# Scores and AV of two head pairs at a time in a sparse-attention and gated-MLP kernel

## The chip, the cores and the metric

The kernel runs on one core of a Trainium2 chip. A core has a matrix engine (TensorE; PE in the profile, with its weight loads as PEld), a vector engine (DVE), a scalar engine for activations (ACT), GpSimd (POOL) and SyncE (SP). Each takes its instructions in its own order and waits for others by semaphores. DMA transfers are issued by SP, ACT and POOL and carried by 16 DMA engines. The metric is the time of one execution in microseconds (us).

## The reference, cut to what matters

For 4 batches, 8 heads, 768 rows and 64 columns: each row attends to the rows less than 16 away and to 24 block summaries (the maximum of the keys and the mean of the values of 32 rows, each with the weight of a whole block). The result goes through a two-layer MLP.

```python
k_sum = k.reshape(B, H, nb, block, D).max(axis=3)          # block 32, nb 24
v_sum = v.reshape(B, H, nb, block, D).mean(axis=3)
scores_l = scale * (q @ k.T)                               # kept where |i - j| < 16
scores_s = scale * einsum('bhsd,bhnd->bhsn', q, k_sum) + log(block)
a = softmax(concat([where(mask_l, scores_l, -1e9), scores_s], -1))
out = a @ concat([v, v_sum], axis=2)
x = out.transpose(0, 2, 1, 3).reshape(B * S, H * D)        # 3072 x 512
h = x @ w_in                                               # 512 -> 2048
y = (h * sigmoid(beta * h)) @ w_out                        # 2048 -> 512
```

## The kernel before, in words

**Attention.** Heads are worked in four pairs (g = 0 to 3), two heads side by side on the partitions. The 768 queries of a head are cut into 12 chunks of 64: six positions m by two parities. A chunk needs only a window of 96 keys, and the 24 summaries stand behind them, so one weight tile `kw[:, par, m]` of 128 columns holds both. The scores of a chunk are one matmul of 128 x 64 per head. An exponential on ACT takes the scores from PSUM to `attn`, a multiplication on DVE with `band` sets what lies outside the window to zero (`mask`), and AV multiplies by `ve` or `vo`: rows of V laid out at an offset for the two parities, a column of ones for the softmax's sum, and the block means in the partitions from 96 on (`mean_v` makes them, `rows_v` copies them in for a pair). `norm` on DVE divides by the sum and writes `x_nat`, and `x_transpose` brings `x_nat` into `xT`, the MLP's input. It does so by PE transposes in batch 0 and for pairs 2 and 3 of batch 1, by a DMA transpose on SP's queue elsewhere.

**MLP.** `h_group` multiplies `w_in` by `xT` (h_ps, then a Silu on ACT), `o_part` multiplies by `w_out` (o_ps, a quarter of a row of 128 tokens at a time, then a copy and a store). Batch 0 is done in two halves (units 0 and 1, 8 h groups each), the others whole (units 2, 3 and 4, 16 groups each).

**PSUM.** Its eight banks are three double banks (tag `big`: scores, AV, h groups) and two single ones (tag `t`: o_ps, some transposes). A buffer is used again when its last reader is done.

**What sets the order.** The program is written out by hand for each engine. Within a batch b the h groups (one each 1.3 of schedule time) and then the o parts (0.865 each) form the main list; `up` is the time at which the o parts begin. Everything else, above all the attention of batch b+1, is put between them with `at_time(t, f, ...)`: a function is written out in front of the first main item whose time is not below t; those with equal t keep the order in which they were named. These are places in the program, not times on the chip. At a batch's end the first two h groups of the next batch begin with three of their four parts (contraction over pairs 0 to 2), and the fourth follows.

**Loads.** Queries, keys and values come by POOL's queue, and after batch 0 also `cross`, which brings keys and queries into place by DMA transposes on SP's queue (`kw`, `qt`); `copy_v` makes `vo` from `ve`. For batches 2 and 3, `load_next` loads a pair's values, keys and queries a whole batch ahead. Its first call also sets a column of `ve` with a memset on DVE, and the large load of values behind it waits for that memset.

Of the kernel before, what the change touches and what calls it, by code (L numbers as in the profile page):

```python
# [12 lines left out]
def kernel(  # L13
# [243 lines left out]
    def kw_of(b, g):  # L257
        return kw_bufs[(b * npair + g) % NKW]
# [109 lines left out]
    def scores_half(g, hf, late=False):  # L368
# [16 lines left out]

        if hf == 0:
            if g % 2 == 0:
                at[(0, g)] = at_pool.tile([P, 2, HM, 2, 2, QT], bf16, name="attn", tag="attn", bufs=3)
            at[(0, g, 0)] = a = at[(0, g - g % 2)][:, g % 2]
            out = a.rearrange("p m h r f -> p h m (r f)")  # L390
            src = big[:, :, 0:2 * HM * QT].rearrange("p h (m f) -> p h m f", f=2 * QT)
        else:
            a = at_pool.tile([P, HM, 2, 2, QT], bf16, name="attn01", tag="attn01", bufs=4)
# [33 lines left out]
    def scores(b, g, par):  # L427
        kw, q = kw_of(b, g), qt_bufs[g]
        if par == 0:
            at[(b, g)] = at_pool.tile([P, 2, nch, 2, QT], bf16, name="attn", tag="attn", bufs=3)  # L430
        a = at[(b, g)][:, par]
        big = ps.tile([P, 2, 512], f32, name="s_ps", tag="big", bufs=3)
        sv = big[:, :, 0:nch * QT].rearrange("p h (m f) -> p h m f", f=QT)
        for m in range(nch):
            for h in range(2):
                lo = h * D
                nc.tensor.matmul(sv[:, h, m], kw[lo:lo + D, par, m, :], q[lo:lo + D, m, par], start=True, stop=True)  # L437
        nc.scalar.activation(out=a.rearrange("p m h f -> p h m f"), in_=sv, func=ACTF.Exp, scale=scale)  # L438

    def mask(b, g, par):  # L440
        a = at[(b, g)][:, par]
        nc.vector.tensor_mul(out=a, in0=a, in1=band[:, par])  # L442

    def av(key, m0, n, tag="big"):
        b, g = key[:2]
        a = at.pop(key)
        if tag == "t":
            o = psum([P, 2, n * VW], f32, "av_ps", "t")
        else:
            o = ps.tile([P, 2, 512], f32, name="av_ps", tag="big", bufs=3)[:, :, 0:n * VW]  # L450
# [177 lines left out]
    for b in range(B):  # L628
# [22 lines left out]
        if nxt == 1:  # L651
            first, step = up + 0.3, 4.4
            for g in pairs:
                t = first + step * g
                p = (up - 9.0, up - 4.5, up + 7.5, up + 8.6)[g]
                if g < 2:
                    at_time(p, prep_k, 1, g, "t")
                    at_time(p + 0.8, prep_q, 1, g, "t", dve)
                    at_time(p + 0.8, copy_v, 1, g)
                else:  # L660
                    at_time(up + 0.5, cross, 1, g)
                    at_time((up + 4.0, up + 6.1)[g - 2], copy_v, 1, g, 0, nch, act)
                at_time(p, top_k, 1, g)
                at_time(p if g < 3 else first + step * 2 + 0.7, rows_k, 1, g)
                for par in range(2):
                    at_time(t, scores, 1, g, par)
                    at_time(t, mask, 1, g, par)
                at_time((up + 2.7, up + 2.7, up + 8.55, first + step * 2 + 0.8)[g], rows_v, 1, g)
                a = t + (4.3 if g == 0 else 3.5)
                at_time(a, av, (1, g), 0, nch)  # L670
                at_time(a, norm, (1, g), nch)
                at_time(a + (0.1 if g < 2 else 2.9), x_transpose, (1, g), 0, nch, "big", dve)
            at_time(up + 2.6, mean_v, 1, pairs, "big")
        elif nxt is not None:
# [10 lines left out]
            for g in range(npair + 1):  # L685
                t = up + 4.0 * g
# [76 lines left out]
```

## Time and profile before

| | us |
|---|---|
| runs of the kernel | 216.63, 216.89, 214.6 (median 216.63) |
| the profiled execution | 214.79, with a span of 213.1 |
| TensorE busy | 206.5 (97%) |
| ACT, DVE, POOL busy | 118.2, 89.4, 66.1 |
| o_ps matmuls (400) | 86.5 busy |
| h_ps matmuls (512) | 86.3 busy |
| scores L437 (288) and AV L455 (336) | 6.3 and 16.8 busy |
| masks L442 (24) | 13.1, 0.556 each |
| exponentials L438 (24) | 18.1, 0.808 each |

Busy times of matmuls overlap, since each is counted from its start to its end and the next begins before that; the chain of work that ended last shows what each adds. In the chain a row gives the start, the length, the engine, the tile and line, and the number of instructions that stand behind each other. In a row of the timeline the brackets at the end give how long the engine was idle before it and who ended that. The landing time of a DMA runs from its issue to its last byte.

By the span's start: batch 0's h groups run to 48.0, its o parts to 74.3; batch 1's h groups from 74.63, batch 2's from 121.13, batch 3's from 167.64.

### The profile page before, as it was taken

The page shows a single profiled execution, that of the slowest core. Times are in us where ns is not written, and L with a number is a line of the kernel's source. Part 1 is how long each engine was busy: PE and PEld are TensorE (multiplying, and loading weights), DVE is VectorE, ACT ScalarE, POOL GpSimd, SP SyncE. Part 2 cuts the span into 40 slices and gives each one's busy share as a digit, 9 for nine tenths or more (in the row PEclk, how much of TensorE's full clock was granted, in tenths as well). Part 3 has the DMA queues.
Part 4 walks back from the last instruction along what each step waited for, and adds up shares of the span by engine and source line. Part 5 has one row for each costly group of instructions (what it writes and reads, how often), then busy time and mean ns, then how long its engine had stood idle before and what let it go on. Part 6 is the DMA issues. An engine that isn't in the chain of part 4 may idle for free.

```text
span 213.1 us, 4886 instructions
## 1 busy us (share of the span) xinstructions
PE 206.5 (97%) x2024; PEld 113.7 (53%) x2024; DVE 89.4 (42%) x233; ACT 118.2 (55%) x165; POOL 66.1 (31%) x88
## 2 busy tenths in 40 slices
PE   7799999999999999999999999999999999999992
PEld 2466666654445565554554455555554556654452
DVE  4487773495798211249644123605454000002121
ACT  3699767879753177668352377678342477740000
POOL 7985345343198483069890000000000000000000
PEclk9999999999999999999999999999999999999999
DMA  6999999999999999999999976721333400001222
GB/s 173 181 154 191 205 204 206 184 178 164 160 133 196 198 221 157 170 150 150 181 150 176 221 156 129 139 40 49 89 86 89 137 0 3 0 0 57 91 86 65
DMA packets 93622, 28.34 MB, mean 133 GB/s; under 512 B 82256, under 2 KB 90656, under 8 KB 93600
## 3 DMA queue, kind: packets, MB, share of 16 engines
q0 software_dynamic: 63184, 13.24, 76.8%
q1 hardware_dynamic: 29968, 14.26, 33.0%
q10 hardware_dynamic: 448, 0.52, 0.7%
q8 instruction: 16, 0.26, 0.5%
q14 instruction: 6, 0.05, 0.1%
HBM read 27.27 MB, written 6.29 MB: 158 GB/s over the span
## 4 chain that ended last, share of the span: by engine, by line
PE 91%; DMA 3%; DVE 2%; issue 1%; POOL 0%; POOLq 0%
PE o_ps L521 40%; PE h_ps L500 39%; PE av_ps L455 4%; DMA q_run<-in_q_dram 3%; PE s_ps L437 3%; PE vm_ps L340 1%; PE px L479 1%; DVE km L293 1%; PE pq L279 1%; PE pk L279 1%; PE av_ps L411 1%; PE av_ps L418 1%; PE s_ps L383 1%; PE beta_ps L332 1%; PE s_ps L378 0%
## 5 line engine op out<-in xcount | busy, mean ns | idle before, releaser
L521 PE MATMUL o_ps<-w_out_sb,h_sb 128*128 128x512 bf16 (+2 forms) x400 | 86.5, 371 | 0.0
L500 PE MATMUL h_ps<-xT,w_in_sb 128*128 128x384 bf16 x512 | 86.3, 326 | 0.0
L507 ACT ACTIVATE h_sb<-h_ps,beta_sb 128x768 bf16<-128x768 f32 (+1 forms) x80 | 59.4, 772 | 24.3 <-PE h_ps L500 24.2
L500 PEld LDWEIGHTS <-w_in_sb 128*128 128x128 bf16 x512 | 49.1, 98 | 32.3 <-issue 0.2
L521 PEld LDWEIGHTS <-h_sb 128*128 128x128 bf16 x400 | 37.0, 98 | 40.9
L541 ACT COPY o_sb<-o_ps 128x512 f32<-128x512 f32 x18 | 10.6, 587 | 31.0 <-PE o_ps L521 19.9
L438 ACT ACTIVATE attn<-s_ps 128x768 bf16<-128x768 f32 x24 | 18.1, 808 | 8.6 <-PE s_ps L437 8.6
L442 DVE TENSOR_TENSOR attn<-attn,band 128x768 bf16<-128x768 bf16 x24 | 13.1, 556 | 20.6 <-ACT attn L438 19.3
L541 DVE COPY o_sb<-o_ps 128x512 f32<-128x512 f32 x5 | 3.5, 692 | 38.5 <-PE o_ps L521 38.5
L118 POOL DMA_DIRECT2D ve<-in_v_dram x12 | 14.4, 1196 | 16.3 <-PE h_ps L500 10.9
L111 POOL DMA_DIRECT2D k_nat<-in_k_dram x20 | 16.8, 843 | 7.5 <-DMA w_out_sb<-in_moe_w_out_dram 4.7
L111 POOL DMA_DIRECT2D q_nat<-in_q_dram x20 | 16.6, 836 | 7.9 <-DMA ve<-in_v_dram 3.8
L465 DVE TENSOR_TENSOR x_nat<-av_ps,r 128x768 bf16<-128x768 f32 (+1 forms) x20 | 15.9, 797 | 0.7
L311 DVE TENSOR_TENSOR half<-kw 128x384 bf16<-128x384 bf16 x8 | 2.9, 358 | 29.8 <-DMA kw<-k_nat 29.8
L293 DVE TENSOR_REDUCE km<-kw 128x24 bf16<-128x768 bf16 x8 | 7.6, 948 | 5.4 <-ACT kw L289 5.3
L464 DVE RECIPROCAL r<-av_ps 128x12 f32<-128x12 f32 (+1 forms) x20 | 4.3, 215 | 10.9 <-PE av_ps L455 9.5
L455 PEld LDWEIGHTS <-attn 128*64 128x64 bf16 x336 | 6.7, 111 | 3.9 <-issue 2.8
L455 PE MATMUL av_ps<-ve,attn 128*64 128x65 bf16 x168 | 8.5, 197 | 0.1
L455 PE MATMUL av_ps<-vo,attn 128*64 128x65 bf16 x168 | 8.3, 197 | 0.0
L437 PEld LDWEIGHTS <-kw 64*128 64x128 bf16 x288 | 4.9, 95 | 4.5 <-issue 4.0
L399 ACT ACTIVATE attn<-s_ps 128x768 bf16<-128x768 f32 x8 | 6.0, 808 | 1.1 <-PE s_ps L383 0.9
L437 PE MATMUL s_ps<-qt,kw 64*128 64x64 bf16 x288 | 6.3, 191 | 0.0
(92 smaller groups left out, 140.1 us busy)
## 6 DMA issues: line engine op xcount, KB each, us to landing
out_dram<-o_sb SPq DMA_DIRECT2D x23, 256.0 KB, 3.0
w_out_sb<-in_moe_w_out_dram POOLq DMA_DIRECT2D x4, 512.0 KB, 17.2
k_nat<-in_k_dram POOLq DMA_DIRECT2D x20, 96.0 KB, 8.2
q_nat<-in_q_dram POOLq DMA_DIRECT2D x20, 96.0 KB, 7.8
w_in_sb<-in_moe_w_in_dram POOLq DMA_DIRECT2D x3, 512.0 KB, 13.4
ve<-in_v_dram POOLq DMA_DIRECT2D x6, 192.0 KB, 7.3
vo<-ve SPq DMA_DIRECT2D x10, 97.5 KB, 5.5
ve<-in_v_dram POOLq DMA_DIRECT2D x2, 384.0 KB, 12.8
```

The costliest lines, as they stand in the source:

```text
L111: nc.gpsimd.dma_start(out=t[:, :, h], in_=(k_row if nm == "k" else q_row)[b, g, :, h])
L118: nc.gpsimd.dma_start(out=ve_bufs[b % 2][:, lo:hi, 0:D], in_=src)
L293: nc.vector.tensor_reduce(out=km_of[g], in_=keys_of(b, g).rearrange("p (n f) -> p n f", f=block), op=ALU.max, axis=mybir.AxisListType.X)
L437: nc.tensor.matmul(sv[:, h, m], kw[lo:lo + D, par, m, :], q[lo:lo + D, m, par], start=True, stop=True)
L438: nc.scalar.activation(out=a.rearrange("p m h f -> p h m f"), in_=sv, func=ACTF.Exp, scale=scale)
L442: nc.vector.tensor_mul(out=a, in0=a, in1=band[:, par])
L455: nc.tensor.matmul(ov[par * QT:(par + 1) * QT, h, m], a[:, par, m, h], t[:, PC * g + nch * h + m0 + m], start=True, stop=True)
L465: nc.vector.tensor_mul(out=x.rearrange("p m h d -> p h m d"), in0=ov[:, :, :, 0:D], in1=r[:, :, :, None].to_broadcast([P, 2, n, D]))
L500: nc.tensor.matmul(big[:, j, 0:MG], w_in_sb[:, ki, ni * P:(ni + 1) * P], xT[b][:, ki, tok:tok + MG], start=(ki == 0), stop=(ki == k1 - 1))
L507: nc.scalar.activation(out=hb.rearrange("p (k m) -> p k m", m=MG), in_=big[:, j:j + w, 0:MG], func=ACTF.Silu, scale=beta_sb[:, ni:ni + 1])
L521: nc.tensor.matmul(o_ps[:, c0:c1], h_bufs[(u, ni * w // k2)][:, ni % (k2 // w), ms * P:(ms + 1) * P], w_out_sb[:, ni, c0:c1], start=(ni == ...
L541: (nc.scalar.copy if u + 1 < len(units) else nc.vector.tensor_copy)(out=o_sb[:], in_=o_ps[:])
```

## The change

Scores of batches 1 to 3 are written for two pairs at once (`scores(b, g0)`): 24 chunks of two heads in three PSUM tiles that fill both banks, and three exponentials of 128 x 1024 in place of four of 128 x 768. `mask` takes a whole pair, 1536 columns, in place of a half. AV of the two pairs of a call follows one on the other, then their two norms. In batch 0 `av_pair` puts AV of two pairs into the two halves of one double bank, where each pair had a single bank. The tiles of `attn` are laid out anew for this (two of four pairs or of two pairs, in place of three and four smaller ones). The times in the schedule change with it, and so do two others: `prep_q` of batch 1 stands next to `prep_k`, and the loads of batch 3 go from 8.0 + 3.5 g to 16.0 + 3.0 g.

```diff
+        if g == 0:
+            at[hf] = at_pool.tile([P, npair, HM, 2, 2, QT], bf16, name="attn", tag="attn", bufs=2)
+        a = at[hf][:, g]
...
-    def scores(b, g, par):
-        kw, q = kw_of(b, g), qt_bufs[g]
-        if par == 0:
-            at[(b, g)] = at_pool.tile([P, 2, nch, 2, QT], bf16, name="attn", tag="attn", bufs=3)
-        a = at[(b, g)][:, par]
-        big = ps.tile([P, 2, 512], f32, name="s_ps", tag="big", bufs=3)
-        sv = big[:, :, 0:nch * QT].rearrange("p h (m f) -> p h m f", f=QT)
-        for m in range(nch):
-            for h in range(2):
-                lo = h * D
-                nc.tensor.matmul(sv[:, h, m], kw[lo:lo + D, par, m, :], q[lo:lo + D, m, par], start=True, stop=True)
-        nc.scalar.activation(out=a.rearrange("p m h f -> p h m f"), in_=sv, func=ACTF.Exp, scale=scale)
+    def scores(b, g0):
+        a = at_pool.tile([P, 2, 2, nch, 2, QT], bf16, name="attn", tag="attn", bufs=2)
+        tiles = [(g, par, m) for g in (g0, g0 + 1) for par in range(2) for m in range(nch)]
+        flat = a.rearrange("p g r m h f -> p (g r m) h f")
+        n = len(tiles) // 3
+        for j in range(3):
+            sv = ps.tile([P, 2, n * QT], f32, name="s_ps", tag="big", bufs=3).rearrange("p h (c f) -> p h c f", f=QT)
+            for c, (g, par, m) in enumerate(tiles[j * n:(j + 1) * n]):
+                for h in range(2):
+                    lo = h * D
+                    nc.tensor.matmul(sv[:, h, c], kw_of(b, g)[lo:lo + D, par, m, :], qt_bufs[g][lo:lo + D, m, par],
+                                     start=True, stop=True)
+            nc.scalar.activation(out=flat[:, j * n:(j + 1) * n].rearrange("p c h f -> p h c f"), in_=sv, func=ACTF.Exp,
+                                 scale=scale)
+        for i in range(2):
+            at[(b, g0 + i)] = a[:, i]
...
+    def av_pair(g0):
+        big = ps.tile([P, 2, 512], f32, name="av_ps", tag="big", bufs=3)
+        for i in range(2):
+            av((0, g0 + i, 1), HM, HM, big[:, i, 0:2 * HM * VW].rearrange("p (h x) -> p h x", h=2))
...
-                t = 2.0 + 2.0 * g
-                at_time(t - 1.4, mask_half, g)
-                at_time(t - 1.4, rows_v, 0, g, HM, nch)
-                at_time(t, av, (0, g, 1), HM, HM, "t")
+                t = 3.9 if g < 2 else 6.5
+                at_time(0.6 + 1.3 * g, mask_half, g)
+                at_time(0.6 + 1.3 * g, rows_v, 0, g, HM, nch)
+                if g % 2 == 0:
+                    at_time(t, av_pair, g)
                 at_time(t, norm, (0, g, 1), HM)
-                at_time(t + 1.9, x_transpose, (0, g, 1), HM, HM, "t", dve)
+                at_time(t + 2.6, x_transpose, (0, g, 1), HM, HM, "t", dve)
...
+            for g0, t, r, a, xt in ((0, up + 0.3, up + 3.4, up + 7.7, 0.1), (2, up + 12.9, up + 12.9, up + 17.2, 2.6)):
+                at_time(t, scores, 1, g0)
+                for f in (rows_v, mask):
+                    for g in (g0, g0 + 1):
+                        at_time(r, f, 1, g)
+                for g in (g0, g0 + 1):
+                    at_time(a, av, (1, g), 0, nch)
+                for g in (g0, g0 + 1):
+                    at_time(a, norm, (1, g), nch)
+                    at_time(a + xt, x_transpose, (1, g), 0, nch, "big", dve)
...
-            for g in range(npair + 1):
-                t = up + 4.0 * g
-                if g < npair:
-                    for par in range(2):
-                        at_time(t, scores, nxt, g, par)
-                        at_time(t, mask, nxt, g, par)
-                if g:
-                    at_time(t, av, (nxt, g - 1), 0, nch)
-                    at_time(t, norm, (nxt, g - 1), nch)
-                    at_time(t, x_transpose, (nxt, g - 1), 0, nch, "big", dve)
+            for g0, t, a in ((0, up + 0.8, up + 5.9), (2, up + 9.0, up + 14.5)):
+                at_time(t, scores, nxt, g0)
+                for g in (g0, g0 + 1):
+                    at_time(t, mask, nxt, g)
+                    at_time(a, av, (nxt, g), 0, nch)
+                for g in (g0, g0 + 1):
+                    at_time(a, norm, (nxt, g), nch)
+                    at_time(a, x_transpose, (nxt, g), 0, nch, "big", dve)
...
-                    at_time(up + 6.0 + 0.01 * (g + 1) if b == 0 else 8.0 + 3.5 * g, load_next, nxt + 1, g)
+                    at_time(up + 6.0 + 0.01 * (g + 1) if b == 0 else 16.0 + 3.0 * g, load_next, nxt + 1, g)
```

Two places in the written order. The first is on DVE, beside batch 1's h groups, in front of the first masks of batch 2. Before, the memset of batch 3's loads (`ve_82`; `ve_81` and `vo_83` belong to batch 2) stood ahead of pair 2's keys (`kw_87`):

```order
L699 MEMSET ve_82 32x48
L311 TENSOR_TENSOR half<-kw_87 128x384
L313 TENSOR_REDUCE km_114<-half 128x24
L319 COPY kw_87<-kw_87 128x6x96
L320 COPY kw_87<-km_114 128x2x6x24
L347 COPY vm_116<-vm_ps 128x130
L353 COPY ve_81<-vm_116 32x780
L353 COPY vo_83<-vm_116 32x780
```

In the change, at the same place of the program:

```order
L320 COPY kw_87<-km_114 128x2x6x24
L347 COPY vm_116<-vm_ps 128x130
L353 COPY ve_81<-vm_116 32x780
L353 COPY vo_83<-vm_116 32x780
L353 COPY ve_81<-vm_116 32x780
L353 COPY vo_83<-vm_116 32x780
L708 MEMSET ve_82 32x48
L353 COPY ve_81<-vm_116 32x780
```

The memset has moved behind pair 2's keys, the mean of the values (`vm_116`) and the copies of two pairs.

The second is SP's queue beside batch 1's o parts, from the second half of batch 2's attention to the first copies for batch 3. Before, a store of an o row stood between two transposes into `xT`:

```order
L474 DMA_TRANSPOSE xT<-x_nat_1936 128x6x128
L542 DMA out_dram<-o_sb 128x512
L474 DMA_TRANSPOSE xT<-x_nat_2017 128x6x128
L542 DMA out_dram<-o_sb 128x512
L474 DMA_TRANSPOSE xT<-x_nat_2071 128x6x128
L542 DMA out_dram<-o_sb 128x512 x2
L328 DMA vo_84<-ve_82 64x780
```

In the change:

```order
L483 DMA_TRANSPOSE xT<-x_nat_1868 128x6x128
L551 DMA out_dram<-o_sb 128x512 x3
L483 DMA_TRANSPOSE xT<-x_nat_2032 128x6x128
L483 DMA_TRANSPOSE xT<-x_nat_2037 128x6x128
L551 DMA out_dram<-o_sb 128x512 x2
L328 DMA vo_84<-ve_82 64x780
```

The transposes of pairs 2 and 3 (the last two into `xT` in each) stand one behind the other, with two stores behind them as the last one had before.

More of the change, by code (lines that the diff above doesn't have):

```diff
@@ L384, in scores_half @@
                              start=True, stop=True, tile_position=(lo, SUM))
+        if g == 0:
+            at[hf] = at_pool.tile([P, npair, HM, 2, 2, QT], bf16, name="attn", tag="attn", bufs=2)
+        a = at[hf][:, g]
         if hf == 0:
[L387 to L389 removed]
+            at[(0, g, 0)] = a
             out = a.rearrange("p m h r f -> p h m (r f)")
@@ L663 @@
                 at_time(p, top_k, 1, g)
-                at_time(p if g < 3 else first + step * 2 + 0.7, rows_k, 1, g)
-                for par in range(2):
[L666 to L673, printed above, removed]
+                at_time(p, rows_k, 1, g)
+            at_time(up + 3.4, mean_v, 1, pairs, "big")
+            for g0, t, r, a, xt in ((0, up + 0.3, up + 3.4, up + 7.7, 0.1), (2, up + 12.9, up + 12.9, up + 17.2, 2.6)):
[8 more added lines that the diff above has]
+                    at_time(a + xt, x_transpose, (1, g), 0, nch, "big", dve)
         elif nxt is not None:
```

21 lines of the change are left out of this document (8 added, 13 removed).

## The prediction

> **What bounds the kernel now.** I read the table of busy times first, then the chain that ended last, in order of time, and then how long single DMAs took to land.
>
> ```profile
> PE 206.5 (97%) x2024; PEld 113.7 (53%) x2024; DVE 89.4 (42%) x233; ACT 118.2 (55%) x165; POOL 66.1 (31%) x88
> ...
> PEclk9999999999999999999999999999999999999999
> ```
>
> TensorE is busy for 97% of the span, its clock granted in full; no other engine passes 55%. Whether it streams or waits, the chain tells (start, length, what, how many matmuls).
>
> ```profile
> 9.10 0.28 PE s_ps L378 x12
> ...
> 25.05 0.31 PE av_ps L455 x12
> 25.36 1.41 PE h_ps L500 x8
> 26.76 0.17 PE px L479 x3
> 26.93 1.30 PE h_ps L500 x8
> 28.23 0.36 PE av_ps L455 x12
> ...
> 30.21 0.52 PE av_ps L455 x12
> ...
> 74.63 14.30 PE h_ps L500 x88
> ...
> 100.93 0.46 PE s_ps L437 x24
> 101.39 0.50 PE av_ps L455 x24
> 101.89 4.42 PE o_ps L521 x20
> ...
> 107.27 3.56 PE o_ps L521 x16
> ...
> 121.13 14.30 PE h_ps L500 x88
> ```
>
> (L378 is scores of batch 0, L437 those of the other batches, L455 AV, L500 the first product h, L521 the second, o; px are transposes.) Two things are to be seen. From 30 us to the end the pieces join without a gap: 88 h matmuls in 14.30 are 0.1625 each at both batches, so there is no wait on that path for the change to remove; only the matmuls themselves and the cost of changing from one kind to another are left. And that cost can be read. For o_ps, 20 matmuls took 4.42 and 16 took 3.56: 0.215 each, and 0.12 more whenever o_ps follows scores or AV. For h_ps, 8 matmuls took 1.41 after AV and 1.30 after px: 0.11. For AV, 24 matmuls took 0.50 and 12 took 0.31: 0.19 for each further dozen, 0.12 for beginning. For scores, 0.46 and 0.28: 0.18 a dozen, 0.10 for beginning. So TensorE gains only by beginning less often, and loses whatever new wait is put into its stream.
>
> **The change part by part.** By these prices 48 AV matmuls in a row cost 0.50 + 2 x 0.19 = 0.88 in place of 2 x 0.50, and 48 scores 0.46 + 2 x 0.18 = 0.82 in place of 2 x 0.46.
>
> *Batch 0.* Four AV pieces (0.31, 0.36, 0.52 and the last like the first, 1.50 in all) become two of 0.50: 0.5 saved. Two returns to h_ps at 0.11 go too, and so does one more with prep_q of pair 1, now next to its prep_k, with its beginning: about 0.4 together. The 0.52 holds a short wait for DVE's rows at 29.9 to 30.2, which goes. I take 1.0. What could be late next: the first av_pair comes at about 25.05 + 1.30 = 26.35 and wants the masks and rows_v of two pairs.
>
> ```profile
> 23.39 0.49 DVE L425 TENSOR_TENSOR attn<-attn,band 128x768 bf16<-128x768 bf16 x1
> 24.82 3.03 ACT L507 ACTIVATE h_sb<-h_ps,beta_sb 128x384 bf16<-128x384 f32 x6 [0.63 <-PE h_ps L500]
> ```
>
> DVE begins them at 23.39; a mask takes about half a microsecond, and the rows_v of half the chunks take at most the 0.65 that a whole pair takes below, so it is through by 23.39 + 2 x 1.15 = 25.7. AV now takes one of the three double banks of the h groups, the one that two Silus of half a microsecond leave at 25.8. Nothing waits for more than 0.1.
>
> *Attention of batch 1* (beside batch 0's o rows). Four scores pieces become two (0.20 saved), four AV become two (0.24), and returns to o_ps, counted along the schedule, fall from eight to five (0.36); 0.8, of which I take 0.7, as one return after px costs nothing before either.
>
> *Attention of batches 2 and 3* (beside the products of batches 1 and 2). Each saves 0.20 and 0.24 as above and one return of five: 0.56.
>
> The sum without any new wait is 1.0 + 0.7 + 2 x 0.56 = 2.8 us.
>
> *ACT and DVE of two pairs.* Two exponentials of 768 took 1.51, 0.76 each; one of 1024 lies between 0.76 and 0.76 x 4/3 = 1.01, and I take 0.90. A mask of 1536 I price as two of 768, which took 1.02.
>
> ```profile
> 97.01 1.28 ACT L438 ACT_TABLE_LOAD   x1
> 98.31 1.51 ACT L438 ACTIVATE attn<-s_ps 128x768 bf16<-128x768 f32 x2
> 102.65 1.02 DVE L442 TENSOR_TENSOR attn<-attn,band 128x768 bf16<-128x768 bf16 x2
> ```
>
> Let X be the start of batch 1's h groups, 74.63 in the trace of before. Batch 2's first scores, now one o piece into the o rows, end at X+23.1, the three exponentials at X+26.4 (the table load ends at X+23.7 as before), and the masks, two of 1.0, the first from the second exponential on, at X+27.6. AV comes six o pieces after scores, at X+23.1+5.28 = X+28.4: 0.8 us of cover. Behind the masks on DVE stand max_k and rows_k of pair 3 (1.5) and then the norms; the norms end at X+31.6, and the next scores want their banks at X+32.9. The o_ps copy of the first row waits behind the exponentials until X+27.0, and its bank is wanted only after X+31. All of that I cost at nothing; if DVE came a microsecond late, AV would wait 0.2 of it, and a second microsecond in full.
>
> *The loads of batch 3.* Here is the part that I do not cost at nothing. The loads are moved from 8.0 to 16.0 of the schedule, and DVE's memset, which frees the tile for the first large load, moves past max_k and rows_k of pair 2, the mean of V and two rows_v.
>
> ```profile
> 91.46 0.10 DVE L699 MEMSET ve<- 32x48 bf16 x1 [0.22 <-issue]
> 92.45 1.05 POOL L118 DMA_DIRECT2D ve<-in_v_dram  x1 [10.94 <-PE h_ps L500]
> 95.95 0.23 DVE L347 CAST vm<-vm_ps 128x130 bf16<-128x130 f32 x1
> ...
> 136.43 0.37 DVE L353 COPY ve<-vm 32x780 bf16<-32x780 bf16 x1
> ...
> 137.08 0.37 DVE L353 COPY ve<-vm 32x780 bf16<-32x780 bf16 x1
> ...
> L111 POOL DMA_DIRECT2D q_nat<-in_q_dram x2: 838/843/848, 110.1 to 110.9; - x2
> DMA to landing us min/median/max: 8.7/8.7/8.8
> ```
>
> Before, the memset at 91.46 let the loads start at 92.45, X+17.8; the last issue, at 110.9, landed 8.8 later, at X+45.1. In the changed order the memset follows the cast (95.95 to 96.18) and the rows_v of two pairs, 0.65 each without POOL beside them (136.43 to 137.08): X+22.9. SP's work for the batch starts 0.3 later against X, as px now stands ahead of the last o part, and a load begins about 1 after its memset: loads from about X+24.2. With the 18.5 us of before from the first issue to the last they are issued until X+42.7 and land until X+51. In that time SP must bring batch 2's x of pairs 2 and 3 into xT by DMA transpose, and batch 2's first h group needs it. How long such a transpose takes to land, beside loads and alone:
>
> ```profile
> L474 SPq DMA_TRANSPOSE xT<-x_nat x1: 1215/1215/1215, 109.9 to 109.9; - x1
> DMA to landing us min/median/max: 7.7/7.7/7.7
> ...
> L474 SPq DMA_TRANSPOSE xT<-x_nat x1: 1212/1212/1212, 118.0 to 118.0; - x1
> DMA to landing us min/median/max: 3.7/3.7/3.7
> ...
> L474 SPq DMA_TRANSPOSE xT<-x_nat x1: 1237/1237/1237, 151.0 to 151.0; - x1
> DMA to landing us min/median/max: 2.7/2.7/2.7
> ...
> L474 SPq DMA_TRANSPOSE xT<-x_nat x1: 2333/2333/2333, 61.0 to 61.0; - x1
> DMA to landing us min/median/max: 8.8/8.8/8.8
> ...
> 116.75 0.23 DVE L464 RECIPROCAL r<-av_ps 128x12 f32<-128x12 f32 x1 [2.36 <-PE av_ps L455]
> 117.02 0.96 DVE L465 TENSOR_TENSOR x_nat<-av_ps,r 128x768 bf16<-128x768 f32 x1
> ```
>
> The last transpose before was issued at 118.01 for a batch that starts at 121.13; it landed in 3.7, as the loads were nearly through, and TensorE never saw it. After the change AV of pairs 2 and 3 starts at X+39.0 (scores at X+32.9, six o pieces on), pair 2's norm takes 0.23 and 0.96 and SP issues its transpose at X+40.8, pair 3's at X+42.1 behind it. That is 16.6 us after the loads began; the row of 109.9 stood 17.5 after them and took 7.7. Seven o pieces after AV batch 2's h groups begin, at X+46.0, and its third matmul, at X+46.3, needs pair 2: 5.5 after the issue. With 7.6 it lands at X+48.4, a **wait of 2.1**; pair 3's, at X+49.7, is then wanted at 48.4 + 10 x 0.1625 = X+50.0 and adds nothing. The ends of this unknown are 2.7 and 3.7 (no wait) and 8.8, the slowest transpose into xT of the trace (3.3 of wait); I take 7.6, from the row nearest in place.
>
> The Trainium skill, "DMA: Bandwidth & Descriptors", section "Queues, rings and completion order", says that a DMA engine serves its queues in turn, a packet from each. By that, beside one other queue a transpose would need about 2 x 2.7 = 5.4, an estimate from the alone row, and the wait would be nil; the row at 109.9 says 7.7, and I go by the row.
>
> At the start of batch 3's h groups no loads run; the 2.7 holds there, and nothing waits.
>
> **Sum.** The profiled execution took 214.79 (span 213.1 and 1.7 around it): 214.79 - 2.8 + 2.1 = 214.1. Two of the three runs shown (216.63 and 216.89) lie about 1.9 above it and one (214.6) beside it, and no view tells what the other kind does. The change has no part in that; I put the forecast halfway, at 214.1 + 0.9 = **215.0**.
>
> **The rivals.**
>
> 1. *The transposes land in time.* Speaks for it: the 3.7 at 118.0, when the last loads were still landing, and that the loads may be through sooner, with batch 2's transposes of keys no longer beside their first ones. Against: the rows of 7.7 and 8.8. It decides at 5.5 us. Time: 214.79 - 2.8 = 212.0, 1.3% faster.
>
> 2. *The transposes land much later, and the change is slower.* Two stand one behind the other in SP's queue, where before an o row lay between. The place is the third matmul of batch 2's h groups; from 8.3 us to landing the wait eats the whole 2.8. With the 12.9 of the slowest load of batch 2 beside its transposes (issued at 80.1), the wait is 40.8 + 12.9 - 46.3 = 7.4 and the time 214.79 - 2.8 + 7.4 = 219.4.
>
> ```profile
> L111 POOL DMA_DIRECT2D q_nat<-in_q_dram x2: 826/832/838, 79.3 to 80.1; - x2
> DMA to landing us min/median/max: 10.3/11.6/12.9
> ```
>
> The Trainium skill, "TensorE: Matmul & The Clock Gate", section "Part 1: The HAM clock gate (the "warmup" mystery)", says that TensorE's clock halves after an idle window of about 3.4 us, which would add to a wait of that length; the granted clock here stays full through all of the trace, and no run shows a longer idle time.
>
> 3. *DVE is late for AV.* The masks of batch 2 stand on DVE behind max_k of pair 2, which waits for a DMA transpose of keys; if that lands 2 us later, the mask of pair 1 ends at X+29.6 and its AV, wanted at X+28.8, waits 0.8.
>
> ```profile
> 94.32 0.36 DVE L311 TENSOR_TENSOR half<-kw 128x384 bf16<-128x384 bf16 x1 [2.76 <-DMA kw<-k_nat]
> ```
>
> For it: such a wait of 2.76 was there. Against: the cover of 0.8 and more. Time: 214.1 + 0.8 = 214.9.
>
> 4. *The merging does nothing* (the beginnings cost as much within a longer run). Then only the wait stays: 214.79 + 2.1 = 216.9, 1% slower. Against it stand the two lengths of each kind.
>
> **How the numbers follow.** A measurement of this kernel tells about 1% from no change. Forecast 0.50 (0.3% faster than before, like against like), rival 1 0.27, rival 2 0.12 (half of it above 1%), rival 3 0.07, rival 4 0.04. Faster by over 1%: rival 1 and a little of the forecast, where the wait comes out under 0.6: 0.28. Slower by over 1%: rivals 2 and 4 in part, and what I have not seen: 0.14. Within 1%: 0.58. The range runs from rival 1 in a low run, 212.0, to the forecast's upper end in a high run: 216.7 - 2.8 + 3.3 = 217.2, widened to 217.6 for rivals 3 and 4; above it lies most of rival 2.
>
> **What would show it.** In the changed profile: scores x48 at about 0.82 and AV x48 at about 0.88 in the chain; three exponentials of 128x1024 at 0.9 each; POOL's load at L118 of batch 3 near six microseconds later against the batch's h groups; the last two transposes into xT landing in over 7; and in the chain, at the start of batch 2's h groups, DMA xT<-x_nat with about 2 us in front of h_ps. If that piece is missing and the time is near 212, rival 1 holds. A chain that goes through DVE masks ahead of AV would prove my cover wrong; o_ps pieces after AV without the 0.12 would prove the prices wrong.

## The result, and the profile after

The changed kernel takes 214.44 us, the median of 16 runs (213.45 to 215.14); the kernel before, run beside it 16 times, takes 215.24 us (214.21 to 217.24). The ratio of the runs is 0.9944, with a 95% interval of 0.9916 to 0.9971: half a per cent faster (the two medians alone give 0.9963). The profiled execution took 213.45 us, the fastest of the 16, and its span is 211.8. A few executions of some kernels are slow as a whole, over 1.5% above the fastest of the same kernel; medians and ratios here and below leave them out.

The rows of the page that answer to those shown of before, busy time of each engine and granted clock:

```profile
PE 202.3 (96%) x2005; PEld 113.3 (54%) x2024; DVE 87.6 (41%) x221; ACT 116.7 (55%) x159; POOL 66.3 (31%) x88
...
PEclk9999999999999999999999999999999999999999
```

TensorE still fills the span, but its share fell by one per cent: it has less work, and a wait that the kernel before did not have. The chain that ended last shows both (start, length, what, how many matmuls):

```profile
63.04 4.26 PE o_ps L530 x19
67.30 0.88 PE av_ps L464 x48
...
72.42 14.30 PE h_ps L509 x88
...
93.89 0.81 PE o_ps L530 x3
94.70 0.81 PE s_ps L438 x48
95.67 5.13 PE o_ps L530 x23
100.80 0.88 PE av_ps L464 x48
...
112.14 0.96 DVE x_nat L474
113.13 7.17 DMA xT<-x_nat
120.34 1.78 PE h_ps L509 x10
122.13 12.51 PE h_ps L509 x76
135.16 6.61 PE h_ps L509 x40
141.82 0.81 PE o_ps L530 x3
```

Scores and AV of two pairs take 0.81 and 0.88 in batches 2 and 3. At the start of batch 2's h groups the chain leaves TensorE: it goes back through a DMA transpose that took 7.17 to the norm that fed it. The waits of TensorE (total, times, longest) and the last two transposes into xT (length of the issue, first and last start, then the time to landing) say the same:

```profile
PE h_ps L509 <- DMA xT<-x_nat: 1.6, 1, 1.6
PE o_ps L530 <- issue: 1.6, 10, 0.2
```

```profile
L483 SPq DMA_TRANSPOSE xT<-x_nat x2: 1217/1276/1336, 113.1 to 114.4; - x2
...
DMA to landing us min/median/max: 7.2/7.4/7.7
```

Stage by stage, read from where the pieces of the two chains begin, and from matmul starts where the chain left TensorE:

| stage | before, us | after, us | difference | predicted |
|---|---|---|---|---|
| start to the first full h groups of batch 0 | 23.67 | 22.93 | -0.74 | 0 |
| batch 0: h groups | 24.37 | 23.45 | -0.92 | -1.0 |
| batch 0: o rows, with batch 1's attention | 26.59 | 26.04 | -0.55 | -0.7 |
| batch 1: h groups | 21.43 | 21.42 | 0 | 0 |
| batch 1: o rows, with batch 2's attention | 25.07 | 24.50 | -0.57 | -0.56 |
| batch 2: h groups | 21.43 | 23.43 | +2.00 | +2.1 |
| batch 2: o rows, with batch 3's attention | 25.08 | 24.52 | -0.56 | -0.56 |
| the rest | 45.51 | 45.46 | 0 | 0 |

The first row is no part of the change: what stands there is not moved. It differs from one execution to the next (22.93 here, 23.51 and 24.07 in the traces of two kernels below that begin in the same way, with the loads early and with the stores on ACT's queue). Without it the profiled execution would gain 0.6.

### The profile page after: what moved, and what is told of

The parts are those of the page before. It is cut to its first block, busy times and chain, and to the rows that moved or that the text cites. A ratio compares the mean times of both kernels' runs of the same rounds, so it can differ in the third digit from the quotient of the medians.

```text
span 211.8 us, 4839 instructions
## 1 busy us (share of the span) xinstructions
PE 202.3 (96%) x2005; PEld 113.3 (54%) x2024; DVE 87.6 (41%) x221; ACT 116.7 (55%) x159; POOL 66.3 (31%) x88
## 4 chain that ended last, share of the span: by engine, by line
PE 84%; DMA 6%; DVE 4%; ACT 2%; issue 2%
PE h_ps L509 40%; PE o_ps L530 30%; DMA xT<-x_nat 3%; PE av_ps L464 2%; DMA kw<-k_nat 2%; PE w_ps L560 2%; PE s_ps L438 2%; DVE x_nat L474 1%; DVE km L293 1%; PE px L488 1%; PE vm_ps L340 1%; ACT attn L440 1%; PE pq L279 1%; PE pk L279 1%; PE s_ps L383 1%
## 5 line engine op out<-in xcount | busy, mean ns | idle before, releaser
L530 PE MATMUL o_ps<-w_out_sb,h_sb 128*128 128x512 bf16 (+2 forms) x383 | 82.9, 370 | 2.0 <-issue 1.6
L530 PEld LDWEIGHTS <-h_sb 128*128 128x128 bf16 x400 | 37.5, 98 | 41.6
L440 ACT ACTIVATE attn<-s_ps 128x1024 bf16<-128x1024 f32 x18 | 17.1, 1024 | 7.0 <-PE s_ps L438 7.0
L447 DVE TENSOR_TENSOR attn<-attn,band 128x1536 bf16<-128x1536 bf16 x12 | 11.1, 957 | 13.5 <-ACT attn L440 13.4
L464 PEld LDWEIGHTS <-attn 128*64 128x64 bf16 x336 | 6.0, 111 | 3.0 <-issue 2.0
L298 DVE COPY qt<-pq 128x768 bf16<-128x768 bf16 x5 | 4.8, 958 | 5.2 <-PE pq L279 5.1
L464 PE MATMUL av_ps<-vo,attn 128*64 128x65 bf16 x168 | 6.8, 196 | 0.0
L464 PE MATMUL av_ps<-ve,attn 128*64 128x65 bf16 x168 | 6.8, 196 | 0.0
L399 ACT ACTIVATE attn<-s_ps 128x768 bf16<-128x768 f32 x8 | 6.1, 808 | 0.7 <-PE s_ps L383 0.6
L560 PE MATMUL w_ps<-warm 128*128 128x512 bf16 x11 | 4.9, 611 | 1.3 <-DVE warm L156 1.3
```

What stands on the lines that cost most here:

```text
L440: nc.scalar.activation(out=flat[:, j * n:(j + 1) * n].rearrange("p c h f -> p h c f"), in_=sv, func=ACTF.Exp, scale=scale)
L447: nc.vector.tensor_mul(out=a, in0=a, in1=band.rearrange("p r m h f -> p (r m h f)"))
L464: nc.tensor.matmul(ov[par * QT:(par + 1) * QT, h, m], a[:, par, m, h], t[:, PC * g + nch * h + m0 + m], start=True, stop=True)
L530: nc.tensor.matmul(o_ps[:, c0:c1], h_bufs[(u, ni * w // k2)][:, ni % (k2 // w), ms * P:(ms + 1) * P], w_out_sb[:, ni, c0:c1], start=(ni == ...
L560: nc.tensor.matmul(w_ps[:, 0], warm[:, 0:P], warm, start=True, stop=True)
```

## The experiments

One measure serves nearly all of them: the time from the first o rows of batch 1 to the first o rows of batch 2, which holds batch 2's attention and batch 2's h groups. Before it is 46.50 (96.06 to 142.56 in the chain). With the 0.56 saved and no wait it should be 45.94; after it is 47.93 (93.89 to 141.82), so the wait costs 2.0. The last two kernels of the table ran beside a kernel before of 215.8 and 216.1 us, the others beside 215.1 to 215.3; the ratio is the column to compare.

| kernel | from, to | stage, us | over 45.94 | median, us | ratio to before, 95% |
|---|---|---|---|---|---|
| changed | 93.89, 141.82 | 47.93 | 1.99 | 214.44 | 0.9944 [0.9916, 0.9971] |
| loads of batch 3 early | 94.61, 141.88 | 47.27 | 1.33 | 214.80 | 0.9976 [0.9946, 1.0007] |
| loads still earlier | 96.41, 144.24 | 47.83 | 1.89 | 214.37 | 0.9967 [0.9932, 1.0002] |
| AV sooner | 94.17, 141.25 | 47.08 | 1.14 | 212.97 | 0.9900 [0.9867, 0.9934] |
| AV sooner, loads early | 94.22, 141.03 | 46.81 | 0.87 | 212.81 | 0.9885 [0.9862, 0.9909] |
| AV sooner, loads still earlier | 94.25, 140.46 | 46.21 | 0.27 | 212.96 | 0.9885 [0.9842, 0.9927] |
| pairs 2, 3 transposed on TensorE | 95.73, 142.35 | 46.62 | 0.68 | 212.67 | 0.9881 [0.9851, 0.9911] |
| without loads of batch 3 | 96.55, 142.50 | 45.95 | 0.01 | 212.85 | 0.9875 [0.9843, 0.9907] |
| stores on ACT's queue | 94.76, 145.00 | 50.24 | 4.30 | 216.68 | 1.0033 [1.0003, 1.0064] |
| without batch 1's stores | 98.60, 145.59 | 46.99 | 1.05 | 213.14 | 0.9882 [0.9806, 0.9958] |

My theory: the new wait is made by batch 3's loads, which the change moved so that they run beside the last two transposes. The first rival: the loads have no part in it, and two transposes one behind the other are slow by themselves.

### Batch 0's part alone, on the kernel before

Edit: the loop of batch 0 (`av_pair`, the masks and `rows_v` at 0.6 + 1.3g, the places of norms and transposes) is taken over; `prep_q` of batch 1 and all of batches 1 to 3 stay as before.

> The kernel before with batch 0's part of the change alone: AV of two pairs into one double bank, and the places of masks, rows_v, norms and transposes of that stage. Theory: batch 0's h stage, 24.4 us in the trace of before, takes about 23.6, since two beginnings of AV, two returns to h_ps and a short wait for DVE go (prep_q stays apart, 0.2 of the 0.9 seen in the changed kernel), and all later stages stay as they were: time 214.5, ratio 0.9965. Rival (what batch 0 gains is taken back by the DMAs behind it, whose times do not move): time 215.2, with a new wait of TensorE in a later stage.

Measured: 214.35 us, 0.9965 [0.9941, 0.9989]. Batch 0's h groups run from 22.98 to 46.60, 23.62 against 24.37: 0.75 in the stage, of the 1.0 that was predicted with `prep_q` beside `prep_k`, and near the 23.6 expected here. This part pays by itself, and brings no wait. The whole change, at 0.9944, is not clear of it: what it saves in batches 1 to 3 (0.55 + 0.57 + 0.56) is less than its new wait of 2.0.

### The loads of batch 3, each kernel with the other's place

Edits: the changed kernel with the loads where they were, and the kernel before with the loads where the change puts them.

```
-  ... else 16.0 + 3.0 * g, load_next, nxt + 1, g)      # changed kernel
+  ... else 8.0 + 3.5 * g, load_next, nxt + 1, g)
```

> The kernel before with only the loads of batch 3 moved to 16.0 + 3.0 g. Theory: the last transpose of batch 2 (pair 3, issued about X+43.4) then lands beside the loads in about 7 us, at X+50.4, and is wanted at X+46.5+1.95 = X+48.4, so that TensorE waits about 2 us and the time rises from 215.2 to about 217.2, a ratio near 1.009. Rival (late loads hurt only where pairs are taken two at a time): no wait in front of batch 2's h groups, time 215.2.

> The changed kernel with the loads of batch 3 back at 8.0 + 3.5 g of the schedule; nothing else differs. Theory (the loads, begun 6 us later, are what the last transposes of batch 2 land beside): the large load of batch 3 begins about X+17.8 again (X the start of batch 1's h groups), the transposes of pairs 2 and 3 into xT land in 6 us or less instead of 7.2 and 7.7, TensorE waits 0 to 0.4 us at the third matmul of batch 2's h groups instead of about 2.0, and the median falls from 214.4 to about 212.6, a ratio to the kernel before near 0.987. Rival (the two transposes are late because they stand one behind the other in SP's queue, loads or not): the wait stays near 2 us and the time near 214.4.

Moving the loads in the kernel before made it slower, as expected: 217.47 us, 1.0103 [1.0072, 1.0134], with the wait in the chain.

```profile
118.32 7.59 DMA xT<-x_nat
125.90 0.04 issue
125.95 12.51 PE h_ps L500 x76
```

So the loads' place alone can make this wait; nothing of the merging is needed. But moving them back in the changed kernel was a miss: 214.80 us instead of the expected 212.6. The wait shrank, and stayed. Chain, and the last two transposes:

```profile
113.89 6.68 DMA xT<-x_nat
120.57 0.04 issue
120.61 14.13 PE h_ps L509 x86
```

```profile
L483 SPq DMA_TRANSPOSE xT<-x_nat x2: 1212/1282/1352, 113.9 to 115.2; - x2
...
DMA to landing us min/median/max: 6.1/6.4/6.7
```

The loads began at X+18.6 (91.74, with X = 73.18), near the X+17.8 of before, and the transposes still took 6.7 (pair 2) and 6.1 (pair 3). TensorE waited for pair 2's. In the kernel before that one was issued at 114.42, X+39.8, and landed in 6.0, at X+45.8, while batch 2's h groups began at X+46.3 (120.97) and needed it with their third matmul. Here it is issued at X+40.7, behind AV of both pairs, and the h groups begin at X+45.8 (118.97). So the merging has a part in the wait too, which I had not given it: it sends pair 2's transpose later, in the middle of the loads, and its use comes sooner.

### AV of two pairs apart again

Edit: on top of the early loads, AV, norm and transpose of the second pair come one o part after the first's in batches 2 and 3.

> The run with early loads, and in attention of batches 2 and 3 AV, norm and transpose of the second pair of each call stand one o part behind those of the first. Theory of the prices (0.12 to begin a run of AV, 0.12 for the return to o_ps): each of the four calls costs 0.24 more, about 1.0 us in all against the run with early loads; in the chain AV x24 at 0.50 twice instead of x48 at 0.88, and one o_ps piece more with its 0.12. Rival (beginning costs nothing, the time lies in the matmuls): AV pieces sum to 0.88 and the time is that of the run with early loads.

215.37 us, 1.0006 [0.9976, 1.0035], 0.57 above the same kernel with AV of two pairs together, where I expected 1.0; these runs cannot tell the two apart. The trace can. The chain, AV of the first two pairs of batch 2:

```profile
102.08 0.50 PE av_ps L464 x24
102.58 0.97 PE o_ps L530 x4
103.55 0.50 PE av_ps L464 x24
104.05 2.70 PE o_ps L530 x12
```

0.97 for four o_ps matmuls is 0.11 over the 0.86 that four take after other o_ps, and AV is begun twice at 0.12. Batch 3's attention, where no loads run, takes 24.97 (143.25 to 168.22) against 24.53: 0.44, by my prices 2 x (0.12 + 0.12) = 0.48. The prices hold there.

### Three ways around the wait

Here I had two theories of how a transpose beside loads behaves: a time from its issue (A), or an end when the loads have drained (B).

```
-  for g0, t, a in ((0, up + 0.8, up + 5.9), (2, up + 9.0, up + 14.5)):
+  for g0, t, a in ((0, up + 0.8, up + 5.9), (2, up + 9.0, up + 12.9)):    # AV sooner
```

> The changed kernel with AV of pairs 2 and 3 of batches 2 and 3 set down at up + 12.9 instead of up + 14.5, two steps of the o stage (1.7 us) sooner; the loads of batch 3 stay at 16.0 + 3.0g. In the changed kernel the masks are done at 109.47 us and AV began at 111.26 us, so AV finds its operands ready at about 109.5, and the last two transposes into xT are issued at about 111.4 and 112.7 us instead of 113.1 and 114.4. Theory A (a transpose beside the loads takes 7.2 to 7.7 us from its issue, whenever it is issued): they land at about 118.7 and 120.4, batch 2's h groups wait at most 0.3 us instead of 1.65, that h stage takes about 21.7 us instead of 23.43, and the median falls by about 1.7 us against the changed kernel (to about 0.987 of the kernel before). Theory B (the transposes end when the loads of batch 3 have drained, at about 120 to 122 us): they take 9 us or more, the wait stays between 1.2 and 1.7 us, and the time stays at 0.994 of before.

> The changed kernel with both: loads of batch 3 at 8.0 + 3.5g as in the kernel before, and AV of pairs 2 and 3 at up + 12.9. Issue of the last two transposes at about 112.2 and 113.5 us. Theory A (the time from issue counts, 6.1 to 6.7 us with loads at this place): landing at 118.9 and 119.6, a wait of at most 0.2 us where early loads alone left 1.2; median about 1.5 us under that kernel, 0.988 to 0.990 of before. Theory B (they end when the loads have drained, about 120 us here): wait of 0.8 us or more, and 0.995 or above.

AV sooner brings 212.97 us, 0.9900 [0.9867, 0.9934], and with early loads 212.81, 0.9885 [0.9862, 0.9909]. Neither theory has it whole. With AV sooner, against the start of the stage the transposes were issued 1.7 sooner, but took 0.8 longer each; the stage got 0.85 shorter:

```profile
L483 SPq DMA_TRANSPOSE xT<-x_nat x2: 1236/1353/1470, 111.7 to 113.0; - x2
...
DMA to landing us min/median/max: 8.0/8.3/8.5
```

```
-  if b > 1 or (b == 1 and g < 2):                      # DMA transpose
+  if b > 2 or (b in (1, 2) and g < 2):                 # pairs 2, 3 of batch 2 on TensorE, 2.6 later
```

> The changed kernel with the outputs of pairs 2 and 3 of batch 2 transposed on TensorE (as batch 1 has it for its pairs 2 and 3), the rest unchanged. Both theories: no wait of batch 2's h groups for a DMA; that h stage falls from 23.43 to about 21.43 us. What is paid: 12 transposes on TensorE, 0.83 us in the row of batch 1, and about 0.1 to 0.25 us for the changes of program around them, so batch 2's attention takes about 25.5 instead of 24.5 us. Net about -1.0 us against the changed kernel, 0.990 of the kernel before. If the h stage keeps more than 0.5 us of the 2.0, the wait was not for the DMA transposes alone.

212.67 us, 0.9881 [0.9851, 0.9911], 1.8 below the changed kernel where I expected 1.0 (by the stage it is 47.93 - 46.62 = 1.3). The wait is gone, and what is paid is only the transposes, with no return price for the o_ps behind them (16 in 3.45 is 0.2156 each):

```profile
114.20 2.54 PE o_ps L530 x11
116.74 0.67 PE px L488 x12
117.41 3.45 PE o_ps L530 x16
120.87 14.30 PE h_ps L509 x88
```

### No loads

Edit: `load_next` for batch 3 loads only k and q of pair 0, which stand in for the other pairs; v stays that of batch 1. The work on the engines is the same. The first sentence on record names the wrong base: the run is the changed kernel, with all four DMA transposes of batch 2.

> The kernel with TensorE transposes is not the base of the reading here: for pairs 2 and 3 of batch 2 it transposes on TensorE. This run leaves out of it all loads of batch 3 except the rows of k and q of pair 0, which stand in for the other pairs, and v stays that of batch 1; the work on the engines is the same. Pairs 0 and 1 of batch 2 still go by DMA transposes. Theory A and B: without loads these two land in under 4 us instead of 6.8 and 8.6, and the last load stands before 104 us. It also shows what the loads cost elsewhere: if the time falls by under 0.5 us against the kernel with TensorE transposes, the loads cost nothing but the wait.

All four transposes of batch 2 landed in 2.7 to 2.8, the last two still one behind the other, and still with output rows before and behind them in SP's queue:

```profile
L483 SPq DMA_TRANSPOSE xT<-x_nat x2: 1212/1225/1238, 115.8 to 117.1; - x2
...
DMA to landing us min/median/max: 2.7/2.8/2.8
```

The stage is 45.95, within 0.01 of what 46.50 - 0.56 gives. So without the loads there is none of the wait, the rival of two transposes in a row falls, and the saving of batch 2's attention is what I had priced. The time, 212.85 us, is not below the 212.67 of TensorE transposes: beyond the wait the loads cost nothing that these runs show.

### Loads still earlier

Edit: `4.5 + 3.5 * g`, so that the memset stands behind the keys of pair 0; alone, and with AV sooner.

> The changed kernel with the loads of batch 3 at 4.5 + 3.5g, so that the memset that opens them stands behind the work for pair 0's keys instead of behind pair 2's (pair 1's, in the kernel before): POOL begins them at about X + 11.5 (84 us) instead of X + 25.9. AV stays at up + 14.5, the last two transposes are issued at about 113 and 114.5 us. Theory B (the transposes are slow as long as packets of the loads remain; loads issued from 90 us had drained by 119 to 120 us): loads from 84 us drain by about 113 to 114 us, these transposes land in 3 to 5 us, and batch 2's h groups do not wait; against the changed kernel the h stage loses 2.0 us. Theory A (7 us from issue as long as the batch has any loads): the wait stays above 1 us. A price that both allow: the loads now run beside the DMA transposes of the keys of pairs 1 to 3 of batch 2, DVE's work on pair 2's keys comes up to 4 us later, its masks with it, and AV of pairs 0 and 1, which had 0.2 us to spare, waits by up to 4 us. By theory B and a price of 1 to 3 us the median is 212.5 to 215.5.

> As the run before, and AV of pairs 2 and 3 at up + 12.9: the last two transposes are issued at about 111.5 and 113 us, so they have 1.7 us more. Theory B: no wait of the h groups (under 0.2 us), and the same price at AV of pairs 0 and 1 as in the run before, so the two times agree within 0.5 us. Theory A: a wait of 0.7 us or more is left, as with loads at 8.0 + 3.5g.

Alone 214.37 us, 0.9967 [0.9932, 1.0002]: no gain over the changed kernel, and a wait of 1.5 in front of h_ps. With AV sooner 212.96, 0.9885 [0.9842, 0.9927], and the wait is down to 0.27 in the stage. The loads began at 86.82 and 85.92, but they had not drained by 114; their packets moved until about 127 and 124. Theory B falls, for the transposes that TensorE waited for landed before that, at 124.5 and 120.7. In the run with AV sooner, packets of both queues from 118 to 120 us (packets, MB, share of 16 engines, which adds up the times of single packets and can pass 100%; the software queue carries the loads, the hardware queue transposes and stores):

```profile
q0 software_dynamic: 847, 0.11, 81.0%
q1 hardware_dynamic: 845, 0.21, 80.3%
```

The price that I had feared at AV of pairs 0 and 1 did not come: AV began 6.9 after the first o piece, as in the changed kernel.

### What a transpose waits for

In the changed kernel the two queues by microsecond show when the transposes' packets move, from 114 to 115 us and from 118 to 119 us:

```profile
q0 software_dynamic: 1009, 0.13, 200.8%
q1 hardware_dynamic: 39, 0.08, 22.9%
...
q1 hardware_dynamic: 418, 0.11, 80.0%
q0 software_dynamic: 417, 0.05, 79.1%
```

39 packets with 0.08 MB are 2 KB each: output rows. 418 with 0.11 MB are some 256 bytes each: the transposes, issued at 113.1, and moving from about 117.7 on, one packet for each packet of the loads. The Trainium skill, "DMA: Bandwidth & Descriptors", section "Queues, rings and completion order", says that a DMA engine takes a packet from each queue in turn; 418 to 417 agrees with it. The 4.6 us from the issue to the first packet are left to explain. Theory C: the transposes wait behind the output rows in one queue.

```
-  nc.sync.dma_start(out=out_r[row], in_=o_sb[:])
+  (nc.scalar if units[u][0] == 1 else nc.sync).dma_start(out=out_r[row], in_=o_sb[:])
```

> The changed kernel with the six stores of batch 1's output rows issued on ACT's queue instead of SP's; loads and AV as in the changed kernel. In the changed kernel the last two transposes, issued at 113.1 and 114.4 us, stand in SP's queue behind output rows issued from 106.2 us on, and the hardware queue moves the small packets of the transposes (some 420 a microsecond) only from 118 us on. Theory C (the transposes wait behind the stores in one queue, and the stores are slow because the loads take turns with them): on a queue of their own the transposes begin about 1.2 us after their issue and share with loads and stores; they land in 3 to 5 us, TensorE's wait of 1.65 us goes (0.3 us at most is left), and the median falls by 1.5 to 2.0 us against the changed kernel, to about 0.987 of before. Theory A (7 us or more beside the loads, whatever stands ahead in the queue): landing 7 to 8 us, the wait stays 1.2 us or more, the time 0.994 of before.

Theory C falls: 216.68 us, 1.0033 [1.0003, 1.0064]. With the stores on a queue of their own (q10) the transposes issued at 114.0 and 115.3 landed in 7.3 and 8.7, and SP's queue moved nothing from 115 to 118 us; these are all rows from 117 to 118:

```profile
q0 software_dynamic: 750, 0.09, 147.2%
q10 hardware_dynamic: 79, 0.16, 46.1%
```

It is slower for a second reason too: ACT could issue its last store only at 124.63, 4.7 us after the copy that fed it (why is not shown), and the Silus stood behind (waits of TensorE, then of ACT):

```profile
PE h_ps L509 <- DMA xT<-x_nat: 2.7, 2, 1.7
...
PE h_ps L509 <- ACT h_sb L516: 1.1, 1, 1.1
...
ACT L516 <- DMA vo<-ve: 5.2, 1, 5.2
```

The last run leaves batch 1's six output rows unwritten (`if units[u][0] != 1:` ahead of the store); the loads stay.

> The changed kernel without the stores of batch 1's six output rows (these rows are left out of the output); loads, AV and transposes as in the changed kernel. With the stores on ACT's queue the packets of the last two transposes still began some 4 us after their issue, while loads and stores moved. Theory D (the 2 KB packets of the stores, 128 in a row, keep the transposes from starting): without them the transposes begin within 2 us of their issue, land in 4 to 5 us, TensorE waits under 0.3 us, and the median is 1.5 to 2 us below the changed kernel. Theory E (the loads' small packets alone do it): landing 6.5 us or more, a wait of 1 us or more, and the median within 0.8 us of the changed kernel.

213.14 us, 0.9882 [0.9806, 0.9958]. The profiled execution is the longest of four (217.07), so only the stage is read from it: 46.99, half of the wait left.

```profile
L483 SPq DMA_TRANSPOSE xT<-x_nat x2: 1212/1238/1265, 117.8 to 119.1; - x2
...
DMA to landing us min/median/max: 5.6/6.2/6.7
```

Neither D nor E has it whole. The four transposes of batch 2 took 6.2, 8.9, 5.6 and 6.7 here, beside loads alone, and 2.7 or 2.8 without the loads (the stores land in 2.0 to 4.0 there). So the loads by themselves make them slow. Packets of the last two begin about 1.8 us after the issue (the first 90 move before 120 us), with stores in flight 4.6 to 4.8, in whichever queue the stores stand. How much of the landing time is due to the stores is not shown, for two reasons: with the loads at their early place the last two took 6.7 and 6.1 beside stores too, and in this execution batch 1's h groups were held up, so that the loads began 1.5 after the first o piece (100.06 and 98.60), where the changed kernel has 4.4. Why stores on another queue should hold back the first packet is open as well.

## Why the prediction was right

**The sum without a wait.** Predicted 2.8, measured 2.6 (0.92 + 0.55 + 0.57 + 0.56). The prices from the lengths of runs, 0.12 to begin AV, 0.10 for scores, 0.12 for the return to o_ps, gave batches 2 and 3 to 0.01, and AV apart gave them back. *Batch 0*: 0.92 for 1.0. *Batch 1*: 0.55 for 0.7, because of a wait of 0.30 that I had costed at nothing (the prices alone gave 0.8). Scores of pairs 2 and 3 took 1.11 there, not 0.81, as DVE's `rows_k` of pair 3 ended only then; in the trace (TensorE, then DVE):

```profile
61.77 1.11 PE L438 MATMUL s_ps<-qt,kw 64*128 64x64 bf16 x48
...
61.67 0.63 DVE L320 COPY kw<-km 128x288 bf16<-128x288 bf16 x1
```

**The new wait.** Predicted 2.1 at the third matmul of batch 2's h groups; measured 2.0 in the stage, 1.65 of it in front of that matmul. The steps: loads from X+24.2, measured X+25.9 (98.27, with X = 72.42); transposes issued at X+40.8 and X+42.1, measured 40.7 and 42.0; landing 7.6, measured 7.2 and 7.7; start of the h groups X+46.0, measured 45.8. The row of 109.9, "nearest in place", was the right kind of row, and the turn-taking of the Trainium skill, taken alone with the 2.7, would have said no wait. That the number came out so near is in part luck: the same two transposes took 8.0 and 8.5 when issued 1.7 sooner. The loads also ran on much longer than I had summed. The last was issued at X+47.5 (119.96), not X+42.7, and the last two took 13.2 and 13.5 to land, past X+60, not X+51; by then TensorE no longer waited. And the reason I gave was only half of it: I put the wait down to the loads' new place, and at their old place two thirds of it stayed.

**Cover on DVE.** I had 0.8 us of it ahead of batch 2's AV; it was 0.2. Masks of both pairs, and the load that opens batch 3's:

```profile
98.74 1.83 DVE L447 TENSOR_TENSOR attn<-attn,band 128x1536 bf16<-128x1536 bf16 x2
...
98.27 1.08 POOL L118 DMA_DIRECT2D ve<-in_v_dram  x1 [16.19 <-PE o_ps L530]
```

They end at 100.57 and AV begins at 100.80. The masks were a little faster than priced (1.83 for 2.0), the three exponentials a little slower (2.85 for 2.7); `max_k` of pair 2 came late, after 5.25 us of waiting for its keys' transpose (2.76 before). Rival 3 was 0.2 us from happening. **Rival 1** (in time, from 5.5 us) needed the loads gone, as the run without them shows. **Rival 2** (8.3 and more) did not come, though pair 1's transpose took 8.6 in the same trace, and 9.9 and 10.3 in other runs (loads still earlier, stores on ACT's queue). **Rival 4** falls with the table of stages.

**The level.** From median to median the change is 0.80 (215.24 to 214.44), and 0.7 was forecast. That 214.44 is 0.6 below my 215.0 comes mostly from the 0.9 that I added for the spread: over 16 runs the kernel before has its median at 215.24, only 0.45 above its profiled 214.79. That is the term that was mis-sized most. The profiled execution, 213.45 for a predicted 214.1, says less: the start alone gave it 0.74. What makes runs differ showed in a place where I had not looked. The executions of 214.12 (no loads) and 215.85 (loads still earlier), above their kernels' medians, have a wait of 1.6 in batch 1's h groups, for batch 2's v. That of 213.61 (transposes on TensorE), also above its median, has none there, but 1.3 for batch 0's v near the start. The profiled executions of before and after have neither. Whether such waits make all of the spread is open.

## What to carry to other kernels

On an engine that is busy for 97%, read the price of changing work from runs of two lengths (twice the matmuls, less than twice the time), and merging can be summed in advance. Then follow every transfer whose issue the merging moves: two results that come out together send their DMAs together, later than the first of them went before, and here that, with the loads moved as well, gave back 2.0 of 2.6. A DMA transpose should be given the time that it takes beside the loads of the hour, not alone; where it can't have that, TensorE does it for 0.34 a pair, or the work ahead of it is set down as soon as its operands are ready.

The four versions that do so, AV sooner (with the loads at each of three places) and transposes on TensorE, take 212.7 to 213.0 us, 0.988 to 0.990 of before. The changed kernel's 0.9944 lies outside their intervals; among themselves they can't be told apart.

## What the hardware showed that I had not expected

- Loads that start sooner need not end sooner. Begun at 98.27 (changed kernel), their packets moved until about 133 us; begun at 91.74 (loads early), until 120; begun at 85.92 and 86.82 (loads still earlier), until about 124 and 127. Beside transposes they moved at 400 to 500 a microsecond, instead of the 1,000 and more that they reach alone.
- Transposes and loads took turns by packet, 418 to 417 and 845 to 847, though the transposes' packets are twice as large (0.11 MB against 0.05). Stores and loads did not, 79 to 750 with the stores on ACT's queue; why is open.
- TensorE's clock was low once behind a short wait. In the profiled execution of the run without stores, the longest of its four, TensorE waited 1.97 us for batch 2's v, with only the 28 small matmuls of the means around it, and the granted clock of the next four microseconds was 0.60 and 0.55 (window, its length, busy time of PE, PEld, DVE, ACT and POOL, clock, DMA share, GB/s):

```profile
90.00:92.00 2.00, 2.00 (x24) 0.98 (x13) 1.11 (x4) 0.00 (x0) 0.00 (x0) 0.60 1.80 97
92.00:94.00 2.00, 2.00 (x9) 0.93 (x8) 0.00 (x0) 0.90 (x1) 0.00 (x0) 0.55 1.67 169
```

  The 40 h matmuls behind it took 8.29 instead of 6.61. Waits of 1.57, 1.64 and 1.65 in other runs left the clock at 1.00, so that this wait lowered it is not shown. The Trainium skill, "TensorE: Matmul & The Clock Gate", section "Part 1: The HAM clock gate (the "warmup" mystery)", puts the idle window at about 3.4 us; this wait was shorter, and one case does not settle where the bound lies.
